# One K load, that of head 16, in three transfers by partitions: 112, 8 and 8

## The chip, the cores and the metric

The kernel runs on one core of a Trainium2 chip. The metric is the time of one execution on the device in microseconds (us), taken over several runs; a profiled execution beside them gives the trace. The core has a matrix engine (TensorE, PE in the profile; its weight loads are PEld), VectorE (DVE), ScalarE (ACT), GpSimd (POOL) and SyncE (SP), which here only issues transfers. Sixteen DMA engines carry data from the device memory (HBM) to the on-chip memory (SBUF), which has 128 partitions.

## The reference

One decode step: layer norm, attention of 32 heads over a cache of 8192 keys, and a gated feed-forward block. All in float32.

```python
B, Sq, D = 1, 1, 640
H, Sk, Dh = 32, 8192, 192
F = 1536
def _A_ref(x, k_cache, v_cache, wq, wo):
    q = (x @ wq) ...                                   # one query a head
    scores = jnp.einsum("bhqd,bhkd->bhqk", q, k_cache) * (Dh ** -0.5)
    p = _softmax(scores, axis=-1)
    o = jnp.einsum("bhqk,bhkd->bhqd", p, v_cache)
    return o.reshape(B, Sq, H * Dh) @ wo
def _B_ref(x, W_gate, W_up, W_down):
    gate, up = x @ W_gate, x @ W_up
    return (gate * (gate > 0) * up) @ W_down
h = x + _A_ref(_layernorm(x), ...)
out = h + _B_ref(_layernorm(h), ...)
```

K and V of a head are 8192 x 192 floats each, 6144 KB; over 32 heads they are 403 MB of the 446 MB that the kernel reads.

## The kernel before

A K or V tile of one head lies in SBUF as 128 partitions of `2 * TW` = 12288 floats (49,152 bytes): partition p holds keys 64p to 64p + 63. The pool `kv` has three such buffers (`kv_t`), which K, V, the query weights and at the end the feed-forward weights share. Every load is issued by SyncE, in the program's order, and a load waits until its buffer is free.

At the start `wq` comes in three transfers and the 32 queries are made. Then the loop over heads: in turn h it loads K of head h + 1, then V of head h (`load_kv`), then works on K of head h + 1 (`head_step`): VectorE multiplies the tile with the query (L183, four parts of 16 keys a partition), GpSimd adds the two halves (L184), VectorE reduces to the scores (L188). The steps of the softmax of head h, whose scores are ready, go between these parts, as do the steps that finish head h - 1. TensorE then takes the values of head h from V (L225, 64 instructions, into `po`). Every four heads a load of `wo` (L91) stands ahead of the K load of that turn; with it the finished heads are added into `acc` (L254).

Since there are three buffers, K of head h + 1 takes the buffer of V of head h - 2 and waits for TensorE; V of head h takes that of K of head h and waits for VectorE's last reduction. Transfers of SyncE use eight semaphores in turn (`DMAHW0` to `DMAHW7` in the listings below), each of which is waited for before it is used again where another wait does not already imply it. The tool that builds the program places these waits; the order on each engine is that of the code.

At the end `w_up`, `w_gate` and `w_down` are loaded into the two freed buffers (L294 to L298, the last in six pieces), and the feed-forward block runs on TensorE with its last product into `pd` (L344), the sum `o` (L347) and the output, four partitions of 640 bytes (L348). V of the last head comes in five pieces by columns.

Of the kernel before, what the change touches and what calls it, by code (L numbers as in the profile page):

```python
# [14 lines left out]
def kernel(  # L15
# [12 lines left out]
    nc = tc.nc  # L28
    P, Q, NQ = 128, 32, 4
    _, H, S, DH = kc.shape  # L30
# [7 lines left out]
    TW = R * DH  # L38
# [11 lines left out]
    kf, vf = kc[0], vc[0]  # L50
# [20 lines left out]
    for j in range(0, DJ, 2):  # L71
        n = min(2, DJ - j)
# [1 line left out]
        nc.sync.dma_start(t3, wq_v[:, j:j + n, :])  # L74
        wq_ts += [t3[:, i, :] for i in range(n)]

    def load_kv(src, h, parts):
        t = kv.tile([P, 2 * TW], F32, name="kv_t")
        v = src[h].rearrange("(p r) d -> p (r d)", p=P)
        b = 0  # L80
        for n in parts:
            nc.sync.dma_start(t[:, b:b + n], v[:, b:b + n])  # L82
            b += n
        return t

    def load_wo(gi):
        hs = GROUPS[gi]
        j = len(hs) * DH // P
        t = wts.tile([P, j, D], F32, tag="wo_t", name="wo_t")
        r0 = hs[0] * DH  # L90
        nc.sync.dma_start(t, wo[r0:r0 + len(hs) * DH, :].rearrange("(p j) n -> p j n", p=P))  # L91
        return t
# [73 lines left out]
    def query(h):  # L166
        g, i = divmod(h, HPQ)
        q = ps_q.tile([P, QB], F32, tag="q", name="q")
        nc.tensor.matmul(q[:, 0:DH], sel[:, g, :], q4[:, i * DH:(i + 1) * DH], start=True, stop=True)  # L169
        return q[:, 0:DH]  # L170
# [5 lines left out]
    def head_step(q, kt, *works):  # L176


        sc = small.tile([P, NS], F32, name="sc")
        k3 = kt.rearrange("p (r d) -> p r d", d=DH)  # L180
        parts = [(i0, k3[:, i0:i0 + SUB, :]) for i0 in range(0, NS, SUB)]
        for i0, ks in parts:
            keep(nc.vector.tensor_mul(ks, ks, q[:, None, :].to_broadcast([P, SUB, DH])))  # L183
            nc.gpsimd.tensor_add(ks[:, :, 0:HD], ks[:, :, 0:HD], ks[:, :, HD:DH])  # L184
            for w in works:
                next(w, None)
        for i0, ks in parts:
            keep(nc.vector.reduce_sum(sc[:, i0:i0 + SUB], ks[:, :, 0:HD], axis=AX.X))  # L188
        return sc

    def softmax_steps(sc, res):
        mp = small.tile([P, 1], F32, name="mp")
        keep(nc.vector.reduce_max(mp, sc, axis=AX.X))  # L193
        pt = ps_s.tile([P, 512], F32, name="ps_small")
        keep(nc.tensor.transpose(pt[0:1, 0:P], mp, ident))  # L195
        yield
        m1 = small.tile([1, 1], F32, name="m1")
        keep(nc.vector.reduce_max(m1, pt[0:1, 0:P], axis=AX.X))  # L198
        pb = ps_s.tile([P, 512], F32, name="ps_small")
        nc.tensor.matmul(pb[:, 0:1], ones[0:1, :], m1, start=True, stop=True)  # L200
        nb = small.tile([P, 1], F32, name="nb")
        nc.scalar.mul(nb, pb[:, 0:1], -SCALE)  # L202
        p = small.tile([P, NS], F32, name="p")
        rs = small.tile([P, 1], F32, name="rs")
        nc.scalar.activation(p, sc, AF.Exp, bias=nb, scale=SCALE, accum_out=rs)  # L205
        pl = ps_s.tile([P, 512], F32, name="ps_small")
        nc.tensor.matmul(pl[:, 0:1], ones, rs, start=True, stop=True)  # L207
        yield
        rl = small.tile([P, 1], F32, name="rl")
        keep(nc.vector.reciprocal(rl, pl[:, 0:1]))  # L210
        res += [p, rl]
        yield
# [8 lines left out]
    def values_of(h, p, rl, vt):  # L221
        po = pos[h % 2]
        for i in range(NP):
            g = i % NQ
            nc.tensor.matmul(po[g * Q:g * Q + 2, :], p[:, 2 * i:2 * i + 2],  # L225
                             vt[:, 2 * i * DH:(2 * i + 2) * DH], start=(i < NQ), stop=(i >= NP - NQ))
        ob = small.tile([P, 2 * DH], F32, name="ob")
        nc.scalar.activation(ob, po, AF.Copy, scale=rl)  # L228
        return ob

    def finish_steps(h, ob, oT, wo_t):

        gi, i = group_of[h]
        U = NQ // len(GROUPS[gi])
        W = DH // U
        pt = ps_s.tile([P, 512], F32, name="ps_small")
        for u in range(U):
            q0 = (i * U + u) * Q
            for k in range(2):
                nc.tensor.matmul(pt[q0:q0 + Q, 0:W], par[:, k, :], ob[:, k * DH + u * W:k * DH + (u + 1) * W],  # L240
                                 start=(k == 0), stop=(k == 1))
        yield
        s = slice(i * U * Q, (i + 1) * U * Q)
        keep(nc.vector.transpose(oT[s], pt[s, 0:W].rearrange("p (c j) -> p j c", c=Q)))  # L244
        yield
        split = h >= H - 2
        if not split and i < len(GROUPS[gi]) - 1:
            return
        if not split:
            s = slice(0, P)  # L250
        J = wo_t.shape[1]
        for j in range(J):
            for g in range(NQ):
                nc.tensor.matmul(acc[g * Q:(g + 1) * Q, :], oT[s, j, :], wo_t[s, j, g * DG:(g + 1) * DG],  # L254
                                 start=False, stop=(h == H - 1 and j == J - 1))
        yield

    sc = head_step(query(0), load_kv(kf, 0, [2 * TW]))
    done = iter(())
    for h in range(H):  # L260
        gi, i = group_of[h]
        if i == 0:
            wo_t = load_wo(gi)
            oT = small.tile([P, len(GROUPS[gi]) * DH // P, Q], F32, tag="oT", name="oT")
        sm = []
        soft = softmax_steps(sc, sm)
        if h + 1 < H:
            kt = load_kv(kf, h + 1, [2 * TW])
            vt = load_kv(vf, h, [2 * TW])
            sc = head_step(query(h + 1), kt, soft, done)  # L270
        else:
            vt = load_kv(vf, h, [TW] + [TW // 4] * 4)
        for w in (soft, done):
            for _ in w:
                pass
        done = finish_steps(h, values_of(h, *sm, vt), oT, wo_t)
# [99 lines left out]
```

## Time and profile before

| | |
|---|---|
| runs | 1045.78 us median of 3 (1045.7 to 1045.9) |
| profiled execution | 1045.67 us, span 1043.9 us |
| busy in the span | DVE 666.0 us, POOL 440.1, PE 409.2, ACT 45.5 |
| DMA | 446.39 MB, 428 GB/s over the span |
| K loads | 32 of 6144 KB, median 37.0 us from issue to landing |
| V loads | 31 of 6144 KB, median 23.1 us |

The span runs from the first to the last instruction. In the page, `out<-in` are the names of the tile written and read, `L183` a line of the kernel; a DMA's share is the part of the time in which the 16 engines had a packet under way, on average. Windows of a few us give shares a little over or under the true ones, because a packet is counted in the window in which it starts. The time from issue to landing holds the wait behind earlier transfers.

### The profile page before, as it was taken

What the parts mean: (1) busy time and instruction counts of PE and PEld (TensorE: products, weight loads), DVE (VectorE), ACT (ScalarE), POOL (GpSimd) and SP (SyncE); (2) the same over time, 40 slices, a digit from 0 to 9 for tenths busy, and PEclk for the clock granted to TensorE, in tenths of its full rate; (3) what the DMA queues carried; (4) which work ended last, traced back from release to release, by engine and by line L of the source; (5) the groups of instructions that cost most, each with busy time, mean ns of one, the idle gap of its engine ahead of it and who ended that gap; (6) DMA issues with size and microseconds to landing.
All of it is one profiled execution on the core that took longest, in us unless ns stands there. A gap on an engine that the chain in (4) does not pass through costs nothing.

```text
span 1043.9 us, 7403 instructions
## 1 busy us (share of the span) xinstructions
PE 409.2 (39%) x3136; PEld 151.0 (14%) x3136; DVE 666.0 (64%) x418; ACT 45.5 (4%) x140; POOL 440.1 (42%) x139
## 2 busy tenths in 40 slices
PE   1603443343345333343432443343233444432475
PEld 0101111111112111121111111121111211111122
DVE  1086777566667766467775666677664667766551
ACT  0000000000000000000000000000000000000010
POOL 0055555344455544245553444455542455544330
PEclk9856665666666566666666666665566666656678
DMA  9999999999999999999999999999999999999997
GB/s 392 445 433 428 424 444 426 435 426 443 426 432 428 439 430 422 438 432 433 428 437 430 435 428 436 429 434 428 433 424 443 430 433 434 428 432 428 435 419 302
DMA packets 13003, 446.39 MB, mean 428 GB/s; under 512 B 1573, under 2 KB 1577, under 8 KB 3114
## 3 DMA queue, kind: packets, MB, share of 16 engines
q1 hardware_dynamic: 12824, 445.92, 99.2%
q8 instruction: 24, 0.39, 0.2%
q14 instruction: 9, 0.07, 0.0%
q10 hardware_dynamic: 146, 0.01, 0.0%
HBM read 445.91 MB, written 0.00 MB: 427 GB/s over the span
## 4 chain that ended last, share of the span: by engine, by line
DMA 62%; DVE 24%; PE 10%; issue 3%; SPq 0%; ACTq 0%; ACT 0%; DVEq 0%
DMA kv_t<-in_A_k_cache_dram 57%; DVE kv_t L183 19%; PE po L225 8%; DVE sc L188 3%; DMA xrow<-in_A_x_dram 2%; DMA ffn_b<-in_B_W_down_dram 2%; DMA ffn_a<-in_B_W_up_dram 2%; PE q L169 1%; PE qp L160 1%; DVE oT L244 1%; DVE m L198 0%; DVE rl L210 0%; DVE mp L193 0%; SPq L82 0%; PE acc L150 0%
## 5 line engine op out<-in xcount | busy, mean ns | idle before, releaser
L184 POOL TENSOR_TENSOR kv_t<-kv_t 128x1536 f32<-128x1536 f32 x128 | 438.2, 3445 | 559.6 <-DVE mp L193 247.4
L183 DVE TENSOR_TENSOR kv_t<-kv_t,q 128x3072 f32<-128x3072 f32 x128 | 427.4, 3342 | 321.1 <-DMA kv_t<-in_A_k_cache_dram 311.5
L225 PE MATMUL po<-kv_t,p 128*2 128x384 f32 x2048 | 224.4, 601 | 9.7 <-DMA kv_t<-in_A_v_cache_dram 9.7
L188 DVE TENSOR_REDUCE sc<-kv_t 128x16 f32<-128x1536 f32 x128 | 215.0, 1739 | 0.0
L195 PE MATMUL ps_small<-ident,mp 128*1 128x128 f32 x32 | 11.8, 368 | 367.6 <-DVE mp L193 367.6
L169 PE MATMUL q<-q,sel 128*128 128x192 f32 x64 | 29.6, 565 | 148.9 <-DVE kv_t L183 148.9
L225 PEld LDWEIGHTS po<-kv_t,p 128*2 128x2 f32 x2048 | 54.7, 97 | 168.9 <-issue 154.3
L195 PEld LDWEIGHTS ps_small<-ident,mp 128*1 128x1 f32 x32 | 2.5, 79 | 389.6 <-issue 355.5
L240 PE MATMUL ps_small<-ob,par 128*32 128x192 f32 (+1 forms) x144 | 44.5, 479 | 0.7 <-ACT ob L228 0.7
L200 PE MATMUL ps_small<-m,ones 1*128 1x1 f32 x64 | 18.4, 354 | 51.9 <-DVE m L198 51.9
L169 PEld LDWEIGHTS q<-q,sel 128*128 128x128 f32 x64 | 14.9, 289 | 156.1 <-DVE kv_t L183 107.5
L228 ACT ACTIVATE ob<-po,rl 128x384 f32<-128x384 f32 x32 | 18.6, 580 | 432.3 <-PE po L225 432.3
L254 PE MATMUL acc<-wo_t,oT 128*32 128x160 f32 (+1 forms) x408 | 33.5, 452 | 0.4 <-DVE oT L244 0.4
L202 ACT ACTIVATE nb<-ps_small 128x1 f32<-128x1 f32 x32 | 5.5, 171 | 495.6 <-PE ps_small L200 495.6
L200 PEld LDWEIGHTS ps_small<-m,ones 1*128 1x128 f32 x64 | 15.7, 303 | 71.8 <-DVE m L198 71.8
L207 PE MATMUL ps_small<-rs,ones 128*128 128x1 f32 x64 | 18.6, 359 | 18.9 <-ACT p L205 18.9
L254 PEld LDWEIGHTS acc<-wo_t,oT 128*32 128x32 f32 (+1 forms) x408 | 18.7, 157 | 6.9 <-DVE oT L244 1.3
L160 PE MATMUL qp<-kv_t,xn 128*32 128x512 f32 x120 | 17.4, 736 | 5.3 <-DMA kv_t<-in_A_wq_dram 4.3
L207 PEld LDWEIGHTS ps_small<-rs,ones 128*128 128x128 f32 x64 | 15.8, 308 | 24.9 <-ACT p L205 24.9
L240 PEld LDWEIGHTS ps_small<-ob,par 128*32 128x32 f32 x144 | 16.7, 153 | 16.9 <-issue 7.5
L244 DVE STREAM_TRANSPOSE oT<-ps_small 32x192 f32<-32x192 f32 (+1 forms) x32 | 11.7, 364 | 10.4 <-PE ps_small L240 9.8
L205 ACT ACTIVATE p<-sc,nb 128x64 f32<-128x64 f32 x32 | 11.1, 348 | 1.0
(72 smaller groups left out, 73.4 us busy)
## 6 DMA issues: line engine op xcount, KB each, us to landing
kv_t<-in_A_k_cache_dram SPq DMA_DIRECT2D x32, 6144.0 KB, 37.0
kv_t<-in_A_v_cache_dram SPq DMA_DIRECT2D x31, 6144.0 KB, 23.1
wo_t<-in_A_wo_dram SPq DMA_DIRECT2D x7, 1920.0 KB, 27.0
kv_t<-in_A_wq_dram SPq DMA_DIRECT2D x2, 6144.0 KB, 17.8
ffn_a<-in_B_W_up_dram SPq DMA_DIRECT2D x1, 3840.0 KB
kv_t<-in_A_wq_dram SPq DMA_DIRECT2D x1, 3072.0 KB, 39.6
kv_t<-in_A_v_cache_dram SPq DMA_DIRECT2D x1, 3072.0 KB, 31.0
kv_t<-in_A_v_cache_dram SPq DMA_DIRECT2D x4, 768.0 KB, 34.6
```

Of the source, the lines that this page charges most:

```text
L160: nc.tensor.matmul(qps[b][g * Q:(g + 1) * Q, :], xn[:, j:j + 1].to_broadcast([P, Q]), wq_ts[j][:, c0:c0 + QB], start=(j == 0), stop=(j == ...
L169: nc.tensor.matmul(q[:, 0:DH], sel[:, g, :], q4[:, i * DH:(i + 1) * DH], start=True, stop=True)
L183: keep(nc.vector.tensor_mul(ks, ks, q[:, None, :].to_broadcast([P, SUB, DH])))
L184: nc.gpsimd.tensor_add(ks[:, :, 0:HD], ks[:, :, 0:HD], ks[:, :, HD:DH])
L188: keep(nc.vector.reduce_sum(sc[:, i0:i0 + SUB], ks[:, :, 0:HD], axis=AX.X))
L200: nc.tensor.matmul(pb[:, 0:1], ones[0:1, :], m1, start=True, stop=True)
L207: nc.tensor.matmul(pl[:, 0:1], ones, rs, start=True, stop=True)
L225: nc.tensor.matmul(po[g * Q:g * Q + 2, :], p[:, 2 * i:2 * i + 2], vt[:, 2 * i * DH:(2 * i + 2) * DH], start=(i < NQ), stop=(i >= NP - NQ))
L228: nc.scalar.activation(ob, po, AF.Copy, scale=rl)
L240: nc.tensor.matmul(pt[q0:q0 + Q, 0:W], par[:, k, :], ob[:, k * DH + u * W:k * DH + (u + 1) * W], start=(k == 0), stop=(k == 1))
L244: keep(nc.vector.transpose(oT[s], pt[s, 0:W].rearrange("p (c j) -> p j c", c=Q)))
L254: nc.tensor.matmul(acc[g * Q:(g + 1) * Q, :], oT[s, j, :], wo_t[s, j, g * DG:(g + 1) * DG], start=False, stop=(h == H - 1 and j == J - 1))
```

## The change

`load_kv` gets a list `ends` of partition bounds, by default one transfer over all 128 partitions. For K of head 16 alone the bounds are 112, 120 and 128, so that load is issued as three transfers, of partitions 0 to 111, 112 to 119 and 120 to 127, one after the other and each over all 12288 columns. All else is as it was.

```diff
-    def load_kv(src, h, parts):
+    def load_kv(src, h, parts, ends=(P,)):
+
         t = kv.tile([P, 2 * TW], F32, name="kv_t")
         v = src[h].rearrange("(p r) d -> p (r d)", p=P)
         b = 0
         for n in parts:
-            nc.sync.dma_start(t[:, b:b + n], v[:, b:b + n])
+            p0 = 0
+            for p1 in ends:
+                nc.sync.dma_start(t[p0:p1, b:b + n], v[p0:p1, b:b + n])
+                p0 = p1
             b += n
         return t
...
-            kt = load_kv(kf, h + 1, [2 * TW])
+            kt = load_kv(kf, h + 1, [2 * TW], [7 * P // 8, 15 * P // 16, P] if h + 1 == H // 2 else [P])
```

On SyncE, the queue of loads from V of head 14 to K of head 18, before (shapes are partitions by floats; in brackets the semaphores waited for; `PE` and `DVE` are those of the engines that free the buffer):

```order
L82 DMA kv_t<-in_A_v_cache_dram 128x12288 [waits DMAHW4_49,DVE_49]
L82 DMA kv_t<-in_A_k_cache_dram 128x12288 [waits DMAHW5_49,PE_49]
L82 DMA kv_t<-in_A_v_cache_dram 128x12288 [waits DMAHW6_49,DMAHW1_49,DVE_49]
L91 DMA wo_t<-in_A_wo_dram 128x3840
L82 DMA kv_t<-in_A_k_cache_dram 128x12288 [waits DMAHW7_49,PE_49]
L82 DMA kv_t<-in_A_v_cache_dram 128x12288 [waits DMAHW0_49,DVE_49]
L82 DMA kv_t<-in_A_k_cache_dram 128x12288 [waits DMAHW1_49,PE_49]
```

And the same stretch of the queue after (three line numbers further on):

```order
L85 DMA kv_t<-in_A_v_cache_dram 128x12288 [waits DMAHW4_49,DVE_49]
L85 DMA kv_t<-in_A_k_cache_dram 112x12288 [waits DMAHW5_49,PE_49]
L85 DMA kv_t<-in_A_k_cache_dram 8x12288 [waits DMAHW1_49]
L85 DMA kv_t<-in_A_k_cache_dram 8x12288
L85 DMA kv_t<-in_A_v_cache_dram 128x12288 [waits DMAHW6_49,DVE_49]
L95 DMA wo_t<-in_A_wo_dram 128x3840
L85 DMA kv_t<-in_A_k_cache_dram 128x12288 [waits DMAHW7_49,PE_49]
L85 DMA kv_t<-in_A_v_cache_dram 128x12288 [waits DMAHW1_49,DMAHW2_49,DMAHW0_49,DVE_49]
```

Nothing changes place: two transfers are put in behind the first, the wait for `DMAHW1` (the load of `wo` for heads 12 to 15) moves from V of head 15 to the first 8-row transfer, and V of head 16, last here, waits for three semaphores of K in place of one. From here on each load has a semaphore two further on.

On VectorE, the first multiply of head 16 and what follows it, before (`sc` are the scores, `mp` and `m` maxima, `oT` a transposed output):

```order
L188 TENSOR_REDUCE sc<-kv_t 128x16 [waits Pool_49] x3
L183 TENSOR_TENSOR kv_t<-kv_t,q 128x3072 [waits DMAHW5_49,DMAHW0_49]
L193 TENSOR_REDUCE mp<-sc 128x1 [waits DVE_49]
L183 TENSOR_TENSOR kv_t<-kv_t,q 128x3072
L198 TENSOR_REDUCE m_1445<-ps_small 1x1 [waits PE_49]
```

and after:

```order
L192 TENSOR_REDUCE sc<-kv_t 128x16 [waits Pool_49] x3
L187 TENSOR_TENSOR kv_t<-kv_t,q 128x3072 [waits DMAHW2_49,DMAHW5_49,DMAHW1_49,DMAHW0_49]
L197 TENSOR_REDUCE mp<-sc 128x1 [waits DVE_49]
L187 TENSOR_TENSOR kv_t<-kv_t,q 128x3072
L202 TENSOR_REDUCE m_1447<-ps_small 1x1 [waits PE_49]
```

The multiply now waits for two more landings; the order is the same, and so is that of PE, ACT and POOL, whose waits for loads name the shifted semaphores.

## The prediction

> **What bounds the kernel now.** I read the page first, its span, DMA lines and chain, and then narrowed the same views to head 16 and to the end. From the page:
>
> ```profile
> span 1043.9 us, 7403 instructions
> DMA  9999999999999999999999999999999999999997
> q1 hardware_dynamic: 12824, 445.92, 99.2%
> DMA 62%; DVE 24%; PE 10%; issue 3%; SPq 0%; ACTq 0%; ACT 0%; DVEq 0%
> ```
>
> The transfers that SyncE issues (q1) keep 16 DMA engines busy for 99.2% of the span; no compute engine is above 64%. The chain agrees: 62% DMA. The table of stretches (last columns: busy share of the DMA engines, GB/s) gives the pace:
>
> ```profile
> core 0: us, PE busy (x) PEld busy (x) DVE busy (x) ACT busy (x) POOL busy (x), PEclk, DMA share, GB/s
> 100.00:950.00 850.00, 329.92 (x2436) 122.26 (x2436) 576.47 (x336) 33.40 (x112) 383.50 (x112) 0.62 1.00 432
> ```
>
> 432 GB/s over 16 busy engines is 27.0 GB/s for each. One partition's row of a K or V tile is 2 * TW floats, 49,152 bytes, so a row costs its engine 1.82 us, and a tile, 8 rows on each engine, 14.6 us. I call 1.82 us a row below.
>
> The chain's pieces near head 16 (start, us, what), VectorE's timeline there and SyncE's issues (start, us) show how far the rest is from mattering:
>
> ```profile
> 512.86 7.23 PE po L225 x64
> 520.11 40.28 DMA kv_t<-in_A_k_cache_dram
> 560.42 3.35 DVE kv_t L183
> ...
> 526.75 3.35 DVE L183 TENSOR_TENSOR kv_t<-kv_t,q 128x3072 f32<-128x3072 f32 x1 [8.31 <-DMA kv_t<-in_A_k_cache_dram]
> ...
> 490.14 0.33 SPq L82 DMA_DIRECT2D kv_t<-in_A_k_cache_dram  x1
> 518.47 0.33 SPq L82 DMA_DIRECT2D kv_t<-in_A_v_cache_dram  x1
> 518.86 0.43 SPq L91 DMA_DIRECT2D wo_t<-in_A_wo_dram  x1
> 520.11 0.33 SPq L82 DMA_DIRECT2D kv_t<-in_A_k_cache_dram  x1
> 547.46 0.33 SPq L82 DMA_DIRECT2D kv_t<-in_A_v_cache_dram  x1
> ```
>
> The load at 490.14 is K of head 16, the one that changes. VectorE starts on it at 526.75 after 8.31 us of idleness. V of head 16 takes its buffer and is issued at 547.46, 20.7 us after the landing. At 526.75 the queue still holds V of head 15, wo and K of head 17 (issued 518.47 to 520.11), 14.6 + 4.5 + 14.6 = 33.7 us of transfers. So compute has some 13 us to spare here, and the end is set by whichever DMA engine finishes its share of rows last.
>
> Do they finish together? At the end, us by us:
>
> ```profile
> 1033.00:1034.00 1.00, 0.21 (x8) 0.21 (x12) 0.73 (x1) 0.00 (x0) 0.00 (x0) 1.00 0.97 389
> 1034.00:1035.00 1.00, 0.81 (x24) 0.47 (x16) 0.00 (x0) 0.00 (x0) 0.00 (x0) 1.00 0.80 325
> 1035.00:1036.00 1.00, 0.59 (x12) 0.50 (x16) 0.00 (x0) 0.00 (x0) 0.00 (x0) 0.76 0.60 246
> 1037.00:1038.00 1.00, 0.44 (x8) 0.20 (x8) 0.00 (x0) 0.00 (x0) 0.00 (x0) 0.50 0.57 223
> 1038.00:1039.00 1.00, 1.00 (x20) 0.77 (x16) 0.00 (x0) 0.00 (x0) 0.00 (x0) 0.53 0.42 161
> 1039.00:1040.00 1.00, 0.87 (x28) 0.43 (x16) 0.00 (x0) 0.00 (x0) 0.00 (x0) 1.00 0.09 36
> ...
> 1040.17 0.52 PE pd L344 x8
> 1040.71 0.38 DVE o L347
> ```
>
> Share times 16 is the number still running: 15.5, 12.8, 9.6, 9.1, 6.7, 1.4. Seven are done by about 1035.5, some 4 to 5.7 us before the last (near 1039.7); the first of the other nine stops near 1038.1, 1.6 us before it. Only then do the last product (1040.17) and the output follow. The nine do not speed up when seven stop (223 GB/s at 0.57 is 24 GB/s each, on short rows). So the ceiling is private to an engine or to its way into SBUF, not the memory that they share.
>
> **The change part by part.** The profiled execution took 1045.67 us, the median of the runs is 1045.78; I sum against 1045.67.
>
> *Which engines move which rows.* Two counts of packets, of 490 to 560 us and of 1041 to 1044 us:
>
> ```profile
> DMA packets 800, 30.20 MB, mean 431 GB/s; under 512 B 96, under 2 KB 96, under 8 KB 96
> ...
> DMA packets 8, 0.00 MB, mean 1 GB/s; under 512 B 4, under 2 KB 8, under 8 KB 8
> ```
>
> In the first, six transfers of 128 partitions land (three of K, two of V, one of wo), with 96 tiny packets: 16 for each, one from each engine. The second is the output of four partitions: four packets under 2 KB but not under 512 B, and four tiny ones. So four rows took four engines, a row each, and were not cut finer. Eight rows should then take eight engines, and 112 rows sixteen with seven each. Eight engines move 7 + 1 + 1 = 9 rows of this tile and the other eight 7, in place of 8 all round: +1.82 us for the first eight, -1.82 us for the rest. Nothing later evens this out, since the share stays at 1.00 to the end: no engine runs short of queued work. Term: **+1.82**.
>
> *Eight engines writing into eight neighbouring partitions.* Before, sixteen engines spread over 128 partitions; now eight write into partitions 112 to 119 at once, and then into 120 to 127. No row shows such a thing, so I bound it. Below: each engine keeps its 1.82 us wherever the row goes, extra 0. Above: a group of partitions takes in no more than its even share of the 432 GB/s, 27 GB/s for eight, so eight rows stand in one line: each transfer takes 8 x 1.82 = 14.6 us in place of 1.82, extra 2 x 7 x 1.82 = 25.5 us. The tail rows (a private ceiling, not a common one) allow both: the limit may sit in the engine or at the partitions. Two in line give 3.64, four 10.92. I take four, the doubling nearest the middle of one and eight: **+10.9**. [...]
>
> *Meeting other traffic there.* While the two small transfers stand in line, the other eight engines go on to V of head 15, which also has rows for partitions 112 to 127. A fifth writer at each place for all of the time would add 2 x 1.82 = 3.64 us, none adds 0; I take half, **+1.8**.
>
> *The 112-row transfer.* Seven rows on an engine need not match the groups that eight matched. From 0 to one more engine in line throughout, 7 x 1.82 = 12.7 us. I take **0**, since seven rows still go to sixteen engines over nearly all partitions, nearest to the 128-row case; the other end is a rival.
>
> *The lead.* The seven early engines, and the first of the other nine, end 1.6 us or more before the last. If the loaded eight are these, the least lead comes off: **-1.6**. If one of the last is among them, 0.
>
> *More transfers.* Two more issues on SyncE, 0.33 us each by the rows above, with 28 us between the issues at 490.14 and 518.47: 0. Inside the queue, the last load of V already comes in five pieces; the stretch over them and one line of the issues:
>
> ```profile
> 998.00:1012.00 14.00, 12.89 (x123) 4.23 (x119) 6.46 (x8) 2.68 (x6) 2.48 (x1) 0.76 1.02 427
> kv_t<-in_A_v_cache_dram SPq DMA_DIRECT2D x4, 768.0 KB, 34.6
> ```
>
> Share 1.02 at 427 GB/s: an extra transfer behind a full queue costs nothing. [...]
>
> *Waits.* The first 8-row transfer waits for the earlier user of its semaphore, a load of wo:
>
> ```profile
> 396.62 0.43 SPq L91 DMA_DIRECT2D wo_t<-in_A_wo_dram  x1
> ```
>
> That one was issued 94 us earlier and has long landed: 0. Were it late, the second small transfer, V of head 15, wo and K of head 17 would queue behind it on SyncE. VectorE's first multiply of head 16 and the issue of V of head 16 now wait for three landings; both come later with the slowest of them. The 13 us to spare covers that, and since the same engines are late with their queue, it moves with them.
>
> Sum: 1.82 + 10.9 + 1.8 + 0 - 1.6 = 12.9; **1045.67 + 12.9 = 1058.6 us**. From +0.2 in the least case to +1.82 + 25.5 + 3.6 = 31 in the worst without the 112-row term. What is late next: the eight loaded engines, until the end; the other eight finish before them, and may run dry now and then at no cost.
>
> **The rivals.**
> A, nothing crowds: the limit sits in the engine, and one row moved is all there is. With the early eight loaded, 1.82 - 1.6 = +0.2: 1045.9 us. With a late one among them +1.82: 1047.5. If every loaded engine leads by more than 1.82 plus the 1.82 that the others lose, the end comes 1.82 us earlier: 1043.9, a shade under 0.2% (2.09 us, about what a measurement of this kernel can tell from no change). For it: the pace was the same in every stretch. It decides from the point where two engines can write neighbouring partitions at full pace. If the eight-row transfers were instead cut over all sixteen engines, 1045.7; the four packets of the output speak against it.
> B, a partial crowd, two in line: 3.64 + 1.82 - 1.6 = +3.9, 1049.5 us. Nothing in the rows sets two apart from four.
> C, the 112-row transfer crowds as well, one more in line for seven rows: 1058.6 + 12.7 = 1071.3 us. Against it: the engines are spread over 112 partitions, not eight.
>
> **How the numbers follow.** Four in line, with a half more or less of the meeting and lead terms, 0.55, its own range 1052 to 1068; A 0.20; B 0.11; C 0.14. Slower by over 0.2% are the first, B and C, 0.80. Within 0.2%: nearly all of A, 0.18; faster 0.02. The range must reach to A on one side, since A and C together are over 0.2; it leaves out C and the fast corner of A: 1045.3 to 1068.
>
> **What would show it.** Right: the two 8-row loads take about 7 us each, with the DMA share still near 1.00 but GB/s in the 520 to 540 us stretch far under 430; the first multiply of head 16 starts near 536, not 526.75; V of head 16 is issued near 557; at the end eight engines run on alone, share near 0.5 for some 8 us. Six landings still leave tiny packets, the eight-row ones eight each. Wrong: GB/s near 430 through 520 to 540 us and a start within 2 us of 526.75 (A); a slow stretch that begins before 520 us (C).

## The result, and the profile after

The changed kernel takes 1069.85 us (median of 4 runs, 1067.67 to 1071.98) against 1045.84 us before (4 runs, 1045.70 to 1045.98): 1.0229 times as long, with an interval of 1.0217 to 1.0241. That is 24.0 us more, for one of the 32 loads of K. The forecast was 1058.6 with a range to 1068.0: slower was right, the size was half of it. The profiled execution took 1068.53 us, 22.9 over the one before.

From the page of the changed kernel, its span, the GB/s of the 40 slices, the queue and the chain:

```profile
span 1066.7 us, 7409 instructions
GB/s 408 418 442 428 437 434 431 425 435 436 430 434 427 437 434 429 431 430 437 244 267 439 432 430 425 439 430 428 432 435 430 430 433 436 431 430 428 435 414 290
q1 hardware_dynamic: 12840, 445.92, 99.2%
DMA 60%; DVE 24%; PE 10%; issue 3%; another core or an unknown queue 3%; SPq 0%; ACTq 0%; ACT 0%; DVEq 0%
```

The engines are as busy as before (99.2%), with the same bytes; two of the 40 slices fall to 244 and 267 GB/s. A busy share cannot show this loss: an engine counts as busy for as long as its packet is under way, however slowly it goes (1.00 at 164 GB/s below). The queue has 16 packets more (12840 against 12824), the completions of two transfers on eight engines each, as the prediction counted them. The stretches over the slow place, of the changed kernel (last columns: busy share, GB/s):

```profile
507.00:530.00 23.00, 7.96 (x66) 2.20 (x66) 11.50 (x7) 0.58 (x1) 8.06 (x3) 0.65 1.02 247
530.00:548.00 18.00, 0.00 (x0) 0.00 (x0) 0.00 (x0) 0.00 (x0) 0.00 (x0) 0.50 1.00 164
```

And of the kernel before:

```profile
507.00:530.00 23.00, 8.19 (x66) 2.25 (x66) 14.69 (x8) 0.58 (x1) 8.03 (x3) 0.65 1.00 432
530.00:548.00 18.00, 10.11 (x75) 3.71 (x75) 17.39 (x12) 0.61 (x3) 13.70 (x4) 0.61 1.00 429
```

At the old pace the bytes of the first stretch would have taken 23 x 247 / 432 = 13.2 us, so 9.8 us are lost there; in the second 18 x (1 - 164 / 429) = 11.1. Together 20.9 of the 22.9 us, all inside 41 us.

VectorE's timeline of the changed kernel (start, us, what; in brackets the idle time before), and below it SyncE's issues:

```profile
548.96 3.35 DVE L187 TENSOR_TENSOR kv_t<-kv_t,q 128x3072 f32<-128x3072 f32 x1 [30.46 <-DMA kv_t<-in_A_k_cache_dram]
```

```profile
491.34 1.09 SPq L85 DMA_DIRECT2D kv_t<-in_A_k_cache_dram  x3
518.53 0.36 SPq L85 DMA_DIRECT2D kv_t<-in_A_v_cache_dram  x1
...
569.67 0.33 SPq L85 DMA_DIRECT2D kv_t<-in_A_v_cache_dram  x1
```

K of head 16 is multiplied from 548.96, not 526.75, and V of head 16 is issued at 569.67, not 547.46: both 22.2 us late. V of head 15 still goes out at 518.53, so no wait on SyncE holds it up. VectorE's 30.46 us of idleness are the 3% that the chain gives to an unknown queue: it does not assign the landings of the three-part load.

The 16 engines signal each landing separately, and the signals, read from the packed trace (no view prints them), split the loss by transfer. The mean and, in brackets, the last signal of each load, in us (16 signals each, but for the 8-row loads):

```
                     before           after
V of head 14         509.8 (512.2)    511.1 (515.7)
K, 112 rows                           535.6 (544.1), the first at 530.9
K, 8 rows, 8 rows                     539.8 (544.6), 545.6 (548.8), of 8 engines each
K of head 16         524.4 (526.7)
V of head 15         539.0 (541.3)    560.2 (563.0)
```

From V of head 14 to the 112 rows are 24.5 us for seven rows, 3.50 us a row against 1.82: 11.8 us too many, and V's own last rows are 1.3 late. The first signal of an 8-row load, at 536.3, follows the first of the 112 rows by 5.4 us, a row's time there (the packet that starts at 530.99 us takes 5.40). From the mean signal of the 112 rows to that of V of head 15 are 24.6 us for nine rows (one of K on the mean, eight of V), 16.4 at full pace: 8.2 too many. So 13.1 us go with the 112-row transfer and 8.2 with the two small ones and V beside them. This is a split by time of landing: until 544.1 us the last engines are still on the 112 rows while others are on the 8-row loads or on V.

### The profile page after: what moved, and what is told of

Read it like the earlier page. It is cut to its first block, busy times and chain, and to the rows that moved or that the text cites. A ratio compares the mean times of both kernels' runs of the same rounds, so it can differ in the third digit from the quotient of the medians.

```text
span 1066.7 us, 7409 instructions
## 1 busy us (share of the span) xinstructions
PE 410.0 (38%) x3136; PEld 151.1 (14%) x3136; DVE 666.0 (62%) x418; ACT 45.6 (4%) x140; POOL 440.2 (41%) x139
## 3 DMA queue, kind: packets, MB, share of 16 engines
q1 hardware_dynamic: 12840, 445.92, 99.2%
## 4 chain that ended last, share of the span: by engine, by line
DMA 60%; DVE 24%; PE 10%; issue 3%; another core or an unknown queue 3%; SPq 0%; ACTq 0%; ACT 0%; DVEq 0%
DMA kv_t<-in_A_k_cache_dram 52%; DVE kv_t L187 19%; PE po L229 8%; DVE sc L192 3%; DMA kv_t<-in_A_v_cache_dram 3%; DMA xrow<-in_A_x_dram 2%; DMA ffn_b<-in_B_W_down_dram 2%; DMA ffn_a<-in_B_W_up_dram 2%; PE q L173 1%; PE qp L164 1%; DVE oT L248 1%; DVE m L202 0%; DVE rl L214 0%; DVE mp L197 0%
## 5 line engine op out<-in xcount | busy, mean ns | idle before, releaser
L199 PE MATMUL ps_small<-ident,mp 128*1 128x128 f32 x32 | 11.8, 368 | 384.2 <-DVE mp L197 384.2
L173 PEld LDWEIGHTS q<-q,sel 128*128 128x128 f32 x64 | 14.6, 284 | 157.1 <-DVE kv_t L187 107.7
L248 DVE STREAM_TRANSPOSE oT<-ps_small 32x192 f32<-32x192 f32 (+1 forms) x32 | 11.7, 364 | 10.4 <-PE ps_small L244 9.7
L209 ACT ACTIVATE p<-sc,nb 128x64 f32<-128x64 f32 x32 | 11.1, 348 | 1.0
```

## The experiments

The theory, W: the pace depends on how many engines write at once into one group of partitions; a group takes in 27 GB/s, what an engine moved before (432 / 16), so two engines at one group ("two in line") go at half pace. Where it takes four neighbours as a group, the four is an assumption that no run tests by itself. Its rivals: B, the uneven rows and nothing else; N, any transfer of fewer than 128 partitions, or more transfers than one, costs; R, the source rows in HBM decide. Each experiment ran once, beside the kernel before on the same chip (1045.66 us for the first four, 1046.39 for the next four, 1045.54 for the rest). The four runs of the changed kernel differ by 4.3 us, so two or three us between experiments are not read. In brackets stands what a run took over its kernel before. A row's time is that of its packet in the packed trace: a row of a tile is one packet of 49,152 bytes. In the first eight, `load_kv` takes a list `sets` of (target partitions, source rows) for K of head 16 alone:

```diff
-            nc.sync.dma_start(t[:, b:b + n], v[:, b:b + n])
+            for d, r in sets or [(slice(0, P), slice(0, P))]:
+                nc.sync.dma_start(t[d, b:b + n], v[r, b:b + n])
```

**Other cuts of the same tile.** First one with 16 rows on sixteen engines, so that all engines have eight rows:

```diff
+            sets = [(slice(a, b), slice(a, b)) for a, b in ((0, 112), (112, 128))]
```

> K of head 16 in two transfers, of 112 and of 16 partitions: the 112-partition transfer of the change stays, and the last 16 rows go to sixteen engines, one row each, so that every engine again has eight rows. Theory W (engines that write into neighbouring partitions at once stand in line): the 112 part costs what it costs in the changed kernel, rows of about 3.5 us in place of 1.82, some +11 us, and the last row of each engine is written beside 15 others into 16 neighbouring partitions, about 5.7 us in place of 1.82, +4 us: 1060 us. Theory B (the cost is the uneven number of rows): nothing is uneven, 1045.7 us. Theory N (every transfer under 128 partitions, or every further transfer, costs the same lump): two such transfers in place of three, +16 us, 1062 us, with no slow stretch of its own for the 112 rows.

1067.88 us, +22.2: as slow as the change, with no uneven rows (B falls), and 7.9 us slower than the 1060 that W gave. Its stretches:

```profile
507.00:530.00 23.00, 8.79 (x66) 2.31 (x66) 11.42 (x7) 0.58 (x1) 7.97 (x3) 0.65 1.03 240
530.00:548.00 18.00, 0.00 (x0) 0.00 (x0) 0.00 (x0) 0.00 (x0) 0.00 (x0) 0.50 0.98 159
```

Again half pace before 530 us. Then three transfers that keep all 128 partitions, of 10752, 768 and 768 columns:

```diff
+            kt = load_kv(kf, h + 1, [10752, 768, 768] if one else [2 * TW])
```

> K of head 16 in three transfers by columns (10752, 768 and 768 of 12288), each over all 128 partitions. Theory W: no crowd, and a further transfer behind a full queue costs nothing: 1045.7 us, within 0.5. Theory B: 1045.7 us. Theory N, in the form that the number of transfers counts: 1069 us as in the changed kernel.

1045.9 us, +0.2. The stretch from 507 to 548 us in this run:

```profile
507.00:548.00 41.00, 17.78 (x137) 5.95 (x141) 32.00 (x19) 1.19 (x4) 21.63 (x7) 0.61 1.00 430
```

430 GB/s: three transfers cost no more than one, so the cut by partitions does it.

**Where the rows go, and where they come from.** Eight transfers of 16 rows each: neighbours, rows 8 apart, and the two crossed. The crossed ones give head 16's keys another order.

```diff
+e3            sets = [(slice(a, a + 16), slice(a, a + 16)) for a in range(0, P, 16)]
+e4            sets = [(slice(a, P, 8), slice(a, P, 8)) for a in range(8)]
+e5            sets = [(slice(16 * a, 16 * a + 16), slice(a, P, 8)) for a in range(8)]
+e6            sets = [(slice(a, P, 8), slice(16 * a, 16 * a + 16)) for a in range(8)]
```

> K of head 16 in eight transfers of 16 neighbouring partitions, one row on each engine every time, so nothing is uneven. Theory W with groups of four neighbours: four engines stand in line for each group throughout; a row takes 5.7 us (as the 8-row transfers showed) to 7.3 us (four times 1.82): 8 x 3.9 to 8 x 5.5 = +31 to +44 us, 1077 to 1090 us. Theory B: 1045.7 us. Theory N: eight transfers, the same time as with partitions eight apart.

> K of head 16 in eight transfers of 16 partitions that are eight apart (a, a + 8, ..., a + 120). Theory W with groups of four neighbours alone: each engine has a group to itself, 1045.7 us. Theory W where the group takes in the four partitions 32 further on as well: two engines stand in line, rows of 3.5 us, 8 x 1.7 = +14 us, 1059 us. Theory B: 1045.7 us. Theory N: the same time as with 16 neighbours.

> As with eight transfers of 16 neighbouring partitions, but each takes rows of the source that are eight apart (the keys of head 16 then stand in another order than its values, so that head's output differs; the work is the same). Theory W (the place in SBUF sets the pace): the time of the 16 neighbours, 1075 us, rows of 4.8 us. Theory R (reading neighbouring rows of the memory sets it): the time of the 16 partitions eight apart, 1065 us, rows of 3.8 us.

> As with eight transfers of 16 partitions that are eight apart, but each takes 16 neighbouring rows of the source (the keys of head 16 in another order than its values, as before). Theory W: 1065 us, rows of 3.8 us. Theory R: 1075 us, rows of 4.8 us.

1074.86 (+29.2), 1065.11 (+19.5), 1071.84 (+25.5) and 1065.61 us (+19.2). The stretch from 509 to 540 us in e3, e4, e5 and e6, in this order:

```profile
509.00:540.00 31.00, 7.71 (x66) 2.15 (x66) 9.22 (x5) 0.58 (x1) 6.15 (x2) 0.61 1.00 161
```

```profile
509.00:540.00 31.00, 8.88 (x66) 2.37 (x66) 9.26 (x5) 0.58 (x1) 6.19 (x2) 0.61 0.99 203
```

```profile
509.00:540.00 31.00, 8.17 (x66) 2.21 (x66) 9.28 (x5) 0.58 (x1) 6.21 (x2) 0.61 1.01 177
```

```profile
509.00:540.00 31.00, 8.69 (x66) 2.30 (x66) 9.49 (x5) 0.58 (x1) 6.43 (x2) 0.61 0.98 202
```

The pace goes with the target: neighbours in SBUF 161 and 177 GB/s, 8 apart 203 and 202, whatever the source rows. R falls. By W, rows 8 apart should have been free if a group were four neighbours only; at half pace (203 and 202 against 432 before), either some partitions 8 or more apart share a group too, or N holds. The neighbours were faster than W has it: 1077 us was the least expected of e3, and four groups at 27 GB/s would be 108 GB/s, not 161. Each of e3's transfers lands over some 9.5 us, which is two rows' time at its 4.85 us a row, so engines are at work in the places of two or three transfers at once. That this is why the pace is above 108 is likely, but not shown. e4 took 6 us more than the 1059 of two in line.

**How far a group reaches.** Sixteen transfers of 8 rows, which eight engines carry: 4 apart within 32 partitions, or 8 apart within 64.

```diff
+e7            sets = [(slice(32 * g + a, 32 * g + 32, 4),) * 2 for g in range(4) for a in range(4)]
+e9            sets = [(slice(64 * g + a, 64 * g + 64, 8),) * 2 for g in range(2) for a in range(8)]
```

> K of head 16 in sixteen transfers of 8 partitions that are four apart (a, a + 4, ..., a + 28, within a block of 32): eight engines carry the whole tile, 16 rows each, the other eight none. Theory W: each of the eight writes into a group of four of its own, so a row takes 1.82 us; the eight are 8 x 1.82 = 14.6 us later, less the lead that they may have (0 to 5.7): 1055 to 1060 us. Theory N (any transfer of less than 128 partitions loses pace, wherever its partitions lie): rows of 3.7 us or more, 16 x 3.7 - 14.6 = +45 us less the lead, 1085 to 1091 us.

> The same sixteen transfers of 8 partitions on eight engines, but eight apart (a, a + 8, ..., a + 56, within a block of 64). Theory W with groups of four neighbours alone: still one engine to a group, 1055 to 1060 us like four apart. Theory W where a group takes in the four partitions 32 further on: two engines to a group, rows of 3.7 us: 1085 to 1091 us. Theory N: as for four apart, 1085 to 1091 us in both.

1070.93 and 1098.47 us. First e7, then e9, each a stretch in which the eight engines run almost alone and one in which V of head 15 has joined on the others:

```profile
511.00:526.00 15.00, 8.11 (x66) 2.20 (x66) 7.39 (x5) 0.58 (x1) 4.36 (x2) 0.73 0.50 214
530.00:545.00 15.00, 0.00 (x0) 0.00 (x0) 0.00 (x0) 0.00 (x0) 0.00 (x0) 0.50 1.00 210
```

```profile
512.00:536.00 24.00, 8.23 (x66) 2.09 (x66) 6.43 (x4) 0.58 (x1) 3.38 (x1) 0.64 0.49 107
545.00:568.00 23.00, 0.00 (x0) 0.00 (x0) 0.00 (x0) 0.00 (x0) 0.00 (x0) 0.50 0.98 147
```

Half the engines (share 0.50) 4 apart move 214 GB/s, eight times 27: by W eight groups, none shared, in transfers of 8 partitions (every row from 511 to 526 us takes 1.82 us, which speaks against N). 8 apart within 64 it is 107, four times 27: two engines to a group. Since 0, 8, 16 and 24 do not share (e7), each of them must share with one of 32, 40, 48 and 56. That it is the one 32 further on is the simplest reading; these runs do not tell it from another pairing.

Both times are above what W gave (1055 to 1060, and 1085 to 1091). Sixteen issues use the eight semaphores twice over, so SyncE was held up by its own loads: V of head 15 went out at 527.00 and 543.60 us, not 518.5, and until then eight engines had nothing to do. Then V met the rest of K: in e7, twice the engines at the same 210 GB/s. These two runs are therefore read by their pace, not by their time.

**The 112 rows and the 8 rows by themselves.** K of head 16 stays whole; behind the K loads of six heads an extra load goes into a buffer that nothing reads. Six loads of 2048 columns are the bytes of one tile's 12288.

```diff
+        t = more.tile([P, 2048], F32, name="more_t")
+        for a, b in ((0, 112),):                # e11: (112, 120), (120, 128); e13: (0, 128)
+            nc.sync.dma_start(t[a:b, :], v[a:b, 0:2048])
...
+            if h + 1 in (6, 10, 14, 18, 22, 26):
+                load_more(h + 1)
```

> The yardstick for the other two: each of the six extra loads is one transfer of 128 partitions, 8 rows of 0.303 us on each engine. Every theory says 6 x 8 x 0.303 = 14.6 us at full pace, 1060.3 us, and GB/s near 430 throughout. More than that would be the price of an extra transfer or of short rows, and comes off the other two.

> K of head 16 is loaded as before, in one transfer. Behind the K loads of six heads (6, 10, 14, 18, 22, 26) one more transfer of 2048 columns and partitions 0 to 111 goes into a buffer of its own that nothing reads; six of them are the bytes of the 112-row transfer. A row is 8192 bytes, 0.30 us at 27 GB/s, seven on each engine: 6 x 7 x 0.303 = 12.7 us at full pace. The prediction's term of 0 for the 112-row transfer says 1045.7 + 12.7 = 1058.4 us and GB/s near 430 throughout. If the transfer by itself runs at the 247 GB/s that the changed kernel shows from 507 to 530 us, it is 12.7 x 432 / 247 = 22.2 us, 1067.9. If it is slow only as long as the 8-row transfers are under way beside it, 1058.4 too.

> As the 112-row run, but each of the six extra loads is two transfers of 8 rows, partitions 112 to 119 and 120 to 127. Six of them are the bytes of the two 8-row transfers of the change. Eight engines with two more rows of 0.303 us each, six times: +3.6 us if nothing crowds, 1049.3. Four in line, as the prediction has it: 3.6 + 10.9 = 14.5, 1060.2. If V behind them meets them as it did in the changed kernel (rows of 5.3 to 6.5 us in place of 1.82 for all engines): 6 x 2 x 0.303 x 3.2 = 11.6, the same within what the leads of the engines (some 2 us) blur. The two runs together stand for the change: 22.2 + 14.5 - 14.6 (the tile's own time) = 22.1 if the 112 rows crowd, 12.6 if not; the change took 24.0.

1060.51 us (+15.0), 1090.81 (+45.3) and 1057.28 (+11.7). The yardstick of 128 partitions came out at its bytes. The 112-row loads cost three times that with an eighth fewer bytes, and no 8-row transfer is near. The extra load behind K of head 14, in the run with 128 partitions and then in that with 112:

```profile
468.00:476.00 8.00, 0.00 (x0) 0.00 (x0) 2.32 (x1) 0.00 (x0) 0.00 (x0) 0.61 1.01 432
```

```profile
474.00:487.00 13.00, 0.00 (x0) 0.00 (x0) 3.33 (x2) 0.00 (x0) 0.00 (x0) 0.52 1.01 285
```

So the 112-row transfer crowds alone. It took more than the expected 1067.9 us, which priced its own rows at 247 GB/s: in the packet records those rows take 0.56 us on the mean, not 0.31, and the rows of K and V that are under way beside them go up to 3 us and more. Of 32.6 us over full pace, 10.4 lie in the extra rows (0.248 us x 672 / 16) and most of the rest in their neighbours. The 8-row loads cost 11.7 us, less than the expected 14.5; 8.1 of it is over their bytes (3.6), about the 8.2 of the split above. The two runs together do not stand for the change, as had been expected: 45.3 + 11.7 - 14.6 = 42.4, where the change took 24.0. Six small loads slow their neighbours six times. So e10 shows that the 112 rows crowd, and not by how much in the change.

**Which transfers of fewer than 128 partitions are slow.** By the simplest reading of e9, with four neighbours as a group, halves of 64 should go two engines to a group and the 64 partitions 32 to 95 one. This also assumes that sixteen engines take equal runs of neighbouring rows, which no trace shows.

```diff
+e12           sets = [(slice(a, a + 64),) * 2 for a in (0, 64)]
+e14           for a, b in ((32, 96),):         # the six extra loads
+e15           for a, b in ((0, 64),):          # the six extra loads
+e16           sets = [(slice(a, b),) * 2 for a, b in ((0, 32), (32, 96), (96, 128))]
```

> K of head 16 in two transfers of 64 partitions, 0 to 63 and 64 to 127, each with four rows on each of sixteen engines, so no engine has more rows than before. If the pace is set by groups of four partitions alone, sixteen groups take in rows of sixteen engines and nothing crowds: 1045.7 us. If a group takes in the four partitions 32 further on as well (32 to 63 share with 0 to 31), eight groups take sixteen engines, two in line, half pace: rows 3.7 us, 14.6 us more, 1060 us, with GB/s near 216 for some 29 us; a few us more where V of head 15 meets the second transfer. If only odd shapes such as 112 are slow, because seven consecutive rows go to an engine, then 64 rows (four to an engine) are free or not by the same groups, and 1045.7 would speak for the odd shape.

> As the run with six extra loads of 112 partitions, but each extra load is one transfer of the 64 partitions 32 to 95. If each of sixteen engines takes four rows that follow one another, and a group that is written through one way is four neighbours with the four 32 further on (both as the runs of 64 and of 8 partitions suggest), then the rows of 32 to 63 and of 64 to 95 go to sixteen different groups, one engine each: full pace, 6 x 4 x 0.303 = 7.3 us, 1045.5 + 7.3 = 1052.8 us (1052 to 1054), GB/s near 430 throughout. If any transfer of fewer than 128 partitions runs at half pace, or the engines lose their order by it: 14.6 us for the rows and some 2 us more for what runs beside each of the six, 1060 to 1075.

> The same with partitions 0 to 63: the same engines, rows and bytes, other places. By groups of four neighbours with the four 32 further on, eight groups take sixteen engines, two in line: 14.6 us for the rows, and beside each of the six the last rows of K and the first of V are slowed too, as they were beside the 112-row loads (1.3 us before and after each, 15.6 in all): 1045.5 + 14.6 + 15.6 = 1076 us (1060 to 1082). If groups were only four neighbours, or the place did not matter, it would be the time of the run with 32 to 95, within 2 us.

> K of head 16 in three transfers, of partitions 0 to 31, 32 to 95 and 96 to 127. By the groups the middle one runs at full pace (four rows of 1.82 us on each engine), the outer two put two engines to a group (two rows each at 3.64 us): 2 x 2 x 1.82 = 7.3 us more, and up to 6 us where the three overlap each other and V: 1053 to 1059, against the 1064.6 of two halves of 64. If every transfer of fewer than 128 partitions is slow for all of its rows: 14.6 us or more, 1060 to 1066.

e12 took 1064.61 us (+19.1), with rows of 3.8 us on the mean from 509 to 540 us: as two in line would give. On these assumptions groups of four neighbours alone are out. It is not only odd shapes such as 112 that are slow (207 GB/s in the same stretch). e14 took 1053.70 (+8.2; its bytes 7.3), e15 1078.08 (+32.5). The stretch around the extra load in e14, and in e15:

```profile
464.00:474.00 10.00, 0.00 (x0) 0.00 (x0) 2.83 (x1) 0.00 (x0) 0.00 (x0) 0.63 1.01 436
```

```profile
472.00:482.00 10.00, 0.00 (x0) 0.00 (x0) 0.70 (x1) 0.00 (x0) 0.00 (x0) 0.51 1.03 268
```

Sixteen engines, four rows on each and the same bytes in both, and only the place differs (with it the source rows, which e5 and e6 had shown not to matter): full pace at 32 to 95, where a row takes 0.313 us on the mean, and not far from half of it at 0 to 63, where it takes 0.564. N falls here, and both times lie within 2.1 us of the forecasts. For e15 the groups gave 14.6 us of that forecast; the other 15.6, for the loads beside it, were taken from e10. e16 took 1064.07 us, where the groups and a bounded overlap gave 1053 to 1059, and N 1060 to 1066. Two stretches of it:

```profile
515.00:523.00 8.00, 7.18 (x60) 1.81 (x64) 3.29 (x2) 0.00 (x0) 0.22 (x1) 0.64 0.89 221
523.00:531.00 8.00, 0.61 (x8) 0.00 (x0) 0.00 (x0) 0.58 (x1) 0.00 (x0) 0.79 1.32 304
```

By the mean landings its middle transfer took 11.5 us for four rows, not 7.3. The first transfer had landed over 8 us (515.4 to 523.3), so late engines were still in it, and early ones in the third, while the middle one ran. From 519 to 531 us a third of the rows take under 2 us and the others up to 5.8. That fits such a mix, but no run holds the engines together to show it. Here a cut with a good place in it gained nothing beside two bad ones. No experiment points to a version faster than the kernel before: where no crowding showed, an engine moved 27 GB/s (214 / 8 in e7, 436 / 16 in e14), which is the old pace.

## Why the prediction was half right

- *The bound and the direction* held. The engines stay 99.2% busy, and what the rows lose comes back at the end: 20.9 us from 507 to 548 us, 22.9 in all. Waits and issues cost nothing here (V of head 15 went out at 518.53, before at 518.47), and nor do further transfers (e2, +0.2 us).
- *Rows and engines* held: 16 packets more, eight landing signals for each 8-row transfer.
- *Eight engines into eight neighbours*, four in line, +10.9, with *meeting other traffic*, +1.8: 12.7 forecast, 8.2 measured for both. No run shows four in line: the second small transfer's row lands 5.8 us after the first's, on the mean, not 7.3; that is 3.2 in line, V included. Sharing at the target was right (177 GB/s in e5, 202 in e6). The dose was picked between bounds and came out half as high again as measured. The first multiply (548.96, not 536) and the issue of V (569.67, not 557) were later than the signs said, by the term below.
- *The 112-row transfer*, "I take 0", is the step that failed. It measured 13.1 us, 1.3 of it in the last rows of V of head 14, near the 12.7 of rival C, which priced one more engine in line throughout. The reason given for 0 was that the engines are spread over nearly all partitions. Being spread is not enough: e10 shows a cost without any 8-row transfer (32.6 us over full pace in six loads), and e14 and e15 show that the place decides for 64 rows. That two engines at a time write into one group in the 112-row transfer too is the author's reading of these runs and not shown; and why nearly all rows then slow, and not those of the two engines alone, is open.
- *Uneven rows less the lead*, +0.2 together: what is left, 22.9 - 13.1 - 8.2 = 1.6 us, is theirs, with the noise of one execution. The eight engines alone at the end did not show:

```profile
1057.00:1058.00 1.00, 0.97 (x24) 0.62 (x24) 0.00 (x0) 0.00 (x0) 0.00 (x0) 1.00 0.82 323
1058.00:1059.00 1.00, 0.50 (x8) 0.40 (x12) 0.00 (x0) 0.00 (x0) 0.00 (x0) 0.69 0.42 166
1059.00:1060.00 1.00, 1.00 (x20) 0.59 (x12) 0.00 (x0) 0.00 (x0) 0.00 (x0) 0.50 0.22 90
```

13, then 7, then 4 engines run (share times 16). V of head 15 already lands spread over 6.5 us with no gap between two sets of eight, so the slow stretch seems to have held up the other engines as much as the eight loaded ones.

- *The sign named for C*, a slow stretch that begins before 520 us, came: rows take 3.2 us and more from 508 to 516 us.

With C's 12.7 in place of 0 the same sum gives the 1071.3 us of that rival, 1.4 over the median and within the four runs. That close is partly luck, since its terms for the small transfers are 4.5 us too high. The chance given to C, 0.14, was too low: nothing in the trace of before said why 128 partitions run at full pace, and that gap should have weighed on every other number of partitions. W's groups fit the paces of two runs: 436 GB/s around e14's load, where they leave each engine one of its own, and 268 around e15's, where they do not. They do not explain the 432 GB/s of 128 partitions: eight neighbours to an engine, with the engines in step, would go two engines to a group there too. Which partitions an engine writes in that transfer, or in the 112-row one, no trace shows; so the 13.1 us of the 112 rows are measured, and not derived from groups.

## What to carry to other kernels

When the DMA engines are the bound, load into all 128 partitions at once and cut by columns: three pieces by columns cost 0.2 us, three by partitions 24.0. A busy share of 1.00 does not say that the engines run at full pace (429 GB/s before and 164 after, from 530 to 548 us); read GB/s beside it, slice by slice. Before costing a transfer of another shape, ask which engines may write into the same group of partitions at the same time (436 GB/s around a load of partitions 32 to 95, 268 around one of 0 to 63), and count the transfers before and behind it too.

## What the runs showed of the hardware

- Eight engines that wrote partitions 4 apart within 32 moved 214 GB/s, 27 each (e7); partitions 8 apart within 64, 107 GB/s, 13 each (e9).
- The place of 64 partitions decided the pace: 436 GB/s around a load of 32 to 95 (e14), 268 around one of 0 to 63 (e15). That a partition shares a group with the one 32 further on is a reading of these runs; the groups themselves stand in no trace.
- Nearly every engine was slow beside a crowded place, also those that carried another load. In e9, once all sixteen run (545 to 568 us), the rows of V of head 15 and of the eight-row loads all take 4.5 to 5.5 us, most of them 5.4, in the packet records; in the changed kernel every row from 508 to 516 us takes 3.2 to 3.65 us, V of head 14 among them. Why is not shown.
- In the changed kernel the slow pace did not last: from 548 us on rows take 1.82 us again, with the engines still 6.5 us apart at the end of V of head 15.
